# Two places a piece in the weight ring between the layers of a two-layer decode kernel

## The chip, the core and the metric

The kernel runs on one core of one Trainium2 chip. The metric is device time in microseconds (us) of one execution.

## The reference

One token for each of two sequences (B = 2, model width 576) goes through attention, MLP, attention, MLP. Both attentions read the same key and value caches and the same weights, and both MLPs the same weights; everything is float32.

```python
# x (2, 1, 576); k_cache, v_cache (2, 32, 8192, 128); wq (576, 4096); wo (4096, 576)
# w_gate, w_up (576, 4608); w_down (4608, 576)
def attention(x):                      # on layernorm(x)
    q = (x @ wq) as 32 heads of 128
    p = softmax(q . k_cache * 128 ** -0.5)
    return (p . v_cache) as 4096 @ wo
def mlp(x):                            # on layernorm(x)
    return (gelu(x @ w_gate) * (x @ w_up)) @ w_down
x = x + attention(layernorm(x)); x = x + mlp(layernorm(x))      # layer 0
x = x + attention(layernorm(x)); x = x + mlp(layernorm(x))      # layer 1
```

## The kernel before

**What is moved.** The two caches hold 537 MB together and are read in each layer, so the kernel is a stream of about 1.15 GB from HBM into one big on-chip tile, `space`. An item is the keys, or the values, of two heads (or of one head for the last four items): 128 partitions by 64 KB or 32 KB. VectorE multiplies keys by the query (L560), GpSimd adds the halves of each product (L577), VectorE sums them (L580), ScalarE takes the exponential (L634), and TensorE multiplies the weights of the softmax by the values (L675). Layer 1 walks the items backwards, and the last keys and values of layer 0 stay on the chip for it.

**Who orders the transfers.** All of them are issued by SyncE in one written order. `plan_first`, `plan_mlp` and `plan_second` append one closure a transfer to `queue`; `pump` lets the head of the list issue as long as `Arena` finds room for it, and `done(key)` frees a piece and calls `pump`. All of this happens while the program is built: in the running program it becomes a semaphore wait in SyncE's queue, in that order, for the instruction that read the old content last.

**The ring.** Between the two streams of caches most of `space` is taken by the held items. Left over are four places of 2304 floats a partition (9216 bytes; 1.18 MB over 128 partitions), which `Arena.ring` hands out in turn. Through these go, in order: `wo` of layer 0 (eight pieces, TensorE L728), the first MLP's gate and up weights (L844), its down weights (L895), and `wq` of layer 1 (L508). Then come keys and values again. In the kernel before, every one of these pieces takes one place, whatever its length up to 2304 floats.

**The first MLP before (`split`).** `norm(split=True)` lays x out so that `split_products(h)` can do half of the 4608 columns at a time: nine pieces for h = 0 (four of gate, one of both, four of up), then `activate(0)`, then nine for h = 1, then `activate(1)`. Each gate or up piece is two DMAs of 64 partitions by 9216 bytes (`split_rows`, L237) or four of 4608 bytes (`split_middle`, L247). The second MLP, at the end, has the whole of `space` and uses `half_rows` (L227) and `all_products` (L858): rows cut in two halves, nine half rows a partition for each of gate and up, both halves of the columns accumulated at once in the two halves of the PSUM tile `acc`. The down weights come in eight pieces of four rows (L260) and one of the four remaining rows (L264).

**TensorE's clock.** TensorE's granted clock in the trace is 1.0 or 0.5. In the last MLP `idle_products` puts products whose result nobody reads between the pieces of the down weights (`IDLE`, L304; L821).

**Names that the steps below use.** `norm` L465, `add_to_x` L497, `attention` L501, `mlp` L826, `activate` L864; tiles `acc`, `bank`, `bank2`, `kept` (PSUM), `prz` (softmax weights), `xt` (transposed x), `hT` (result of the activation).

Of the kernel before, what the change touches and what calls it, by code (L numbers as in the profile page):

```python
# [15 lines left out]
P = 128  # L16
# [51 lines left out]
class Arena:  # L68
# [31 lines left out]

    def ring(self, key, n):

        at = self.take(key, RING + self.turn % NPLACE * PLACE, n)
        self.turn += at is not None
        return at

    def fit(self, key, n, lo=0):
# [15 lines left out]
def decode_layers(ctx, tc, x_in, kc, vc, wq, wo, wg, wu, wd, out):  # L123
# [28 lines left out]
    def done(key):  # L152
        arena.free(key)
        pump()
# [73 lines left out]

        weights(key, len(us) * width, first, transfers)

    def split_rows(name, w, h, u):

        rows = w[:, DF // 2 * h:DF // 2 * (h + 1)].rearrange("(m r) w -> m r w", r=NU)

        def transfers(t):
            for e in range(2):
                nc.sync.dma_start(t[e::2, :], rows[:, 5 * e + u, :])  # L237

        weights((name, 0, h, u), DF // 2, None, transfers)

    def split_middle(h):

        def transfers(t):
            for g, w in enumerate((wg, wu)):
                for e in range(2):
                    lo, n = DF // 4 * (2 * h + e), DF // 4
                    nc.sync.dma_start(  # L247
                        t[e::2, n * g:n * (g + 1)], w[:, lo:lo + n].rearrange("(m r) w -> m r w", r=NU)[:, 4, :]
                    )

        weights(("gu", 0, h), DF // 2, None, transfers)

    def down(layer, rows):

        (t0, i0), (t1, i1) = rows[0], rows[-1]
# [23 lines left out]
    def out_rows(layer, g):  # L279
# [9 lines left out]
        weights(("wo", layer, g), GH * D, whole_at[layer], transfers)  # L289


    single = [range(u, u + 1) for u in range(NU)]
    three = [range(u, u + 3) for u in range(0, NU, 3)]
    WQ = [three, single]
    GU = [three, three[:-1] + single[-3:]]

    DOWN = [
        [[(t, i) for i in range(lo, lo + 4)] for t in range(NT) for lo in (0, 4)] + [[(t, NI - 1) for t in range(NT)]],
        [[(t, i) for i in range(NI)] for t in range(NT - 2)]
        + [[(NT - 2, i) for i in range(lo, hi)] for lo, hi in ((0, 5), (5, 9))]  # L300
        + [[(NT - 1, i) for i in range(lo, hi)] for lo, hi in ((0, 3), (3, 6), (6, 8), (8, 9))],
    ]

    IDLE = (4, 4, 2, 2, 1)  # L304

    whole_at = (None, 0)
    def groups(layer):
# [68 lines left out]
            out_rows(1, g)  # L376

    def plan_mlp(layer):
        if layer == 0:
            for h in range(2):  # L380
                for u in range(4):
                    split_rows("g", wg, h, u)
                split_middle(h)
                for u in range(4):
                    split_rows("u", wu, h, u)
        else:
            for g, (name, w) in enumerate((("g", wg), ("u", wu))):
                for us in GU[g]:
                    half_rows((name, layer, us[0]), w, us, 0)
        for rows in DOWN[layer]:  # L390
            down(layer, rows)

# [44 lines left out]
    )  # L437

    xt = consts.tile([P, PAD + NU * 32], F32, name="xt")
    nc.vector.memset(xt, 0.0)

# [18 lines left out]
        return smalls[0][0:p, 0:n]  # L462


    def norm(split=False):  # L465
# [11 lines left out]
        xr = x.rearrange("p (m r) -> p r m", r=NU)  # L477
        xs = xc.rearrange("p w s -> p (w s)")
        if split:
            xm = xs[:, :5 * 32].rearrange("p (u m e) -> p u m e", u=5, e=2)  # L480
            parts = [(xm[:, 0:4, :, e], xr[:, 5 * e:5 * e + 4, :], 0) for e in range(2)]
            parts += [(xm[:, 4, :, e], xr[:, 4, :], e) for e in range(2)]
            xs = xs[:, :5 * 32].rearrange("p (u q) -> p u q", u=5)
        else:
            parts = [(xc[:, :, s], x, s) for s in range(2)]
            xs = xs.rearrange("p (q u) -> p u q", u=NU)
        for to, of_x, s in parts:
            nc.vector.tensor_scalar(to, of_x, mv[:, 0:1], side[:, s:s + 1], op0=ALU.subtract, op1=ALU.mult)
        u = xs.shape[1]
        nc.vector.transpose(xt[:, PAD:PAD + 32 * u].rearrange("p (u q) -> p u q", u=u), xs)  # L490
# [7 lines left out]
        nc.vector.tensor_add(x, xps, x)  # L498


    def attention(layer):  # L501
        rstd = norm()

        for us in WQ[layer]:
            w = ready.pop(("wq", layer, us[0])).rearrange("p (u c w) -> p u c w", c=4, w=EQ)
            for u in us:
                for c in range(4):
                    nc.tensor.matmul(  # L508
                        acc[32 * c:32 * c + 2 * B, 0, :], xt[:, PAD + 32 * u:PAD + 32 * u + 2 * B],
                        w[:, u - us[0], c, :], start=(u == 0), stop=(u == NU - 1),  # L510
                    )
            done(("wq", layer, us[0]))
        qsb = once.tile([P, EQ], F32, name="qsb", tag="row")

        qb, S, prod, rs, mT, tot, rinv, osb = {}, {}, {}, {}, {}, {}, {}, {}
# [300 lines left out]
            project(g)  # L816
        add_to_x()

    def idle_products(n):
        for _ in range(n):  # L820
            nc.tensor.matmul(  # L821
                kept.rearrange("p j d -> p (j d)")[0:4, :HG], ident[:, 0:4], xt[:, :HG], start=True, stop=True,
            )


    def mlp(layer):  # L826
        split = layer == 0
        rstd = norm(split)
        hT = once.tile([P, 2, NI, 2, 2, B], F32, name="hT", tag="xc")

        def window(u, at):

            return xt[:, PAD + 32 * u - at:PAD + 32 * u - at + 4 * B]

        def split_products(h):

            steps = [(("g", layer, h, u), u, 2, (0,)) for u in range(4)] + [(("gu", layer, h), 4, 1, (0, 1))]
            steps += [(("u", layer, h, u), u, 2, (1,)) for u in range(4)]
            for key, u, sides, gs in steps:
                w = ready.pop(key).rearrange("p (k c w) -> p k c w", c=4, w=HG)  # L840
                for k in range(2):
                    g, e = (k, 0) if u == 4 else (gs[0], k)
                    for c in range(4):
                        nc.tensor.matmul(  # L844
                            acc[32 * c:32 * c + 4 * B, h, :HG], window(u, 4 * g + 2 * e), w[:, k, c, :],
                            start=(key == steps[0][0] and k == 0), stop=(key == steps[-1][0] and k == 1),
                        )
                done(key)

        def all_products():  # L850

            for g, name in enumerate("gu"):
                for us in GU[g]:
                    w = ready.pop((name, layer, us[0])).rearrange("p (u v c w) -> p u v c w", v=2, c=4, w=HG)
                    for u in us:
                        for v in range(2):
                            for c in range(4):
                                nc.tensor.matmul(  # L858
                                    acc[32 * c:32 * c + 4 * B, v, :HG], window(u, 4 * g), w[:, u - us[0], v, c, :],
                                    start=(g == 0 and u == 0), stop=(g == 1 and u == NU - 1),  # L860
                                )
                    done((name, layer, us[0]))

        def activate(v):  # L864

# [13 lines left out]
            nc.vector.tensor_scalar_mul(to[:, :, 0, :], a, 0.5)  # L879
            nc.scalar.mul(to[:, :, 1, :], a, 0.5)  # L880

        if not split:
            all_products()
        for v in range(2):
            if split:
                split_products(v)
            activate(v)
        for n, rows in enumerate(DOWN[layer]):
            if layer == 1 and n < len(IDLE):
                idle_products(IDLE[n])  # L890
            w = ready.pop(("d", layer, rows[0])).rearrange("p (i c) -> p i c", c=D)
            for k, (t, i) in enumerate(rows):
                v, e = divmod(t, 2) if split else (t % 2, t // 2)
                for c in range(4):
                    nc.tensor.matmul(  # L895
                        xps[32 * c:32 * c + 2 * B, :], hT[:, v, i, e, :, :].rearrange("p s b -> p (s b)"),
                        w[:, k, c * CW:(c + 1) * CW],
                        start=(rows is DOWN[layer][0] and k == 0), stop=(t, i) == (NT - 1, NI - 1),
                    )
            done(("d", layer, rows[0]))  # L900
# [35 lines left out]
```

## Time and profile before

| what | value |
|---|---|
| median of three executions | 2691.84 us (2690.37 to 2692.72) |
| profiled execution | 2692.85 us |
| its span, first to last instruction | 2691.1 us |
| read from HBM | 1153.18 MB, 429 GB/s over the span |
| busy: TensorE, VectorE, GpSimd, ScalarE | 34%, 69%, 45%, 5% |
| chain that ended last | DMA 85%, VectorE 12% |
| mean granted TensorE clock | 0.629 |

The time around the span, 1.75 us, is in the profiled execution's time and not in its span. The traced execution stands 1.0 us above the median. The page divides the span into 40 slices of 67 us; the change lies in slices 19 to 21, from about 1260 to 1420 us. The granted clock is a record of its own in the trace, in stretches whose lengths are multiples of 3.41 us.

### The profile page before, as it was taken

What the parts mean: (1) busy time and instruction counts of PE and PEld (TensorE: products, weight loads), DVE (VectorE), ACT (ScalarE), POOL (GpSimd) and SP (SyncE); (2) the same over time, 40 slices, a digit from 0 to 9 for tenths busy, and PEclk for the clock granted to TensorE, in tenths of its full rate; (3) what the DMA queues carried; (4) which work ended last, traced back from release to release, by engine and by line L of the source; (5) the groups of instructions that cost most, each with busy time, mean ns of one, the idle gap of its engine ahead of it and who ended that gap; (6) DMA issues with size and microseconds to landing.
All of it is one profiled execution on the core that took longest, in us unless ns stands there. A gap on an engine that the chain in (4) does not pass through costs nothing.

```text
span 2691.1 us, 18230 instructions
## 1 busy us (share of the span) xinstructions
PE 923.9 (34%) x7046; PEld 300.5 (11%) x7046; DVE 1851.1 (69%) x1688; ACT 144.6 (5%) x736; POOL 1214.7 (45%) x550
## 2 busy tenths in 40 slices
PE   1323332332233233334654333233233323332346
PEld 0100010000001010111211101001010101010022
DVE  4877787678777776867038778777777877787740
ACT  0000000000000000000016000000000000000000
POOL 2644454455445444544018554445444544454420
PEclk7656655665666566666766665666566556656678
DMA  9999999999999999999999999999999999999998
GB/s 421 435 437 433 432 432 433 431 436 433 432 436 432 434 427 434 433 430 425 408 402 425 433 435 429 436 430 433 436 433 432 431 437 432 431 433 435 434 421 368
DMA packets 33831, 1154.36 MB, mean 429 GB/s; under 512 B 4024, under 2 KB 4048, under 8 KB 5840
## 3 DMA queue, kind: packets, MB, share of 16 engines
q1 hardware_dynamic: 33704, 1153.19, 99.7%
q8 instruction: 55, 0.90, 0.1%
q14 instruction: 32, 0.26, 0.0%
q10 hardware_dynamic: 40, 0.01, 0.0%
HBM read 1153.18 MB, written 0.00 MB: 429 GB/s over the span
## 4 chain that ended last, share of the span: by engine, by line
DMA 85%; DVE 12%; PE 1%; POOL 1%; ACT 1%; issue 1%; SPq 0%; ACTq 0%; POOLq 0%; DVEq 0%
DMA space<-in_A_k_cache_dram 77%; DVE space L560 7%; DVE S L580 4%; DMA space<-in_B_w_up_dram 2%; DMA space<-in_B_w_down_dram 2%; DMA space<-in_A_v_cache_dram 1%; DMA space<-in_A_wo_dram 1%; DMA space<-in_B_w_gate_dram 1%; POOL space L577 1%; DMA space<-in_A_wq_dram 1%; ACT space L570 0%; POOL space L564 0%; DMA x<-in_A_x_dram 0%; PE bank L895 0%; PE acc L844 0%
## 5 line engine op out<-in xcount | busy, mean ns | idle before, releaser
L577 POOL TENSOR_TENSOR space<-space 128x1024 f32<-128x1024 f32 (+1 forms) x510 | 1181.4, 2316 | 1208.0 <-DVE space L560 1197.3
L560 DVE TENSOR_TENSOR space<-space,bank 128x2048 f32<-128x2048 f32 (+1 forms) x512 | 1153.7, 2254 | 608.4 <-DMA space<-in_A_k_cache_dram 574.8
L675 PE MATMUL acc<-space,prz 128*8 128x512 f32 x4096 | 596.6, 746 | 451.9 <-DMA space<-in_A_v_cache_dram 447.8
L580 DVE TENSOR_REDUCE S<-space 128x16 f32<-128x1024 f32 (+1 forms) x512 | 610.1, 1192 | 3.5 <-POOL space L577 3.3
L528 PE MATMUL bank<-qsb,pick 4*64 4x128 f32 (+1 forms) x256 | 46.6, 437 | 776.5 <-DVE space L560 773.8
L675 PEld LDWEIGHTS acc<-space,prz 128*8 128x8 f32 x4096 | 119.2, 104 | 872.0 <-DMA space<-in_A_v_cache_dram 450.0
L632 ACT ACTIVATE nbs<-bank 64x1 f32<-64x1 f32 (+1 forms) x128 | 21.1, 165 | 2256.5 <-PE bank L611 2255.8
L528 PEld LDWEIGHTS bank<-qsb,pick 4*64 4x64 f32 (+1 forms) x256 | 20.9, 202 | 835.0 <-DVE space L560 803.7
L700 PE MATMUL bank<-of,osb 128*32 128x2 f32 x512 | 40.9, 202 | 130.9 <-DVE osb L691 130.9
L611 PE MATMUL bank<-m,unit 1*128 1x2 f32 (+1 forms) x136 | 39.0, 354 | 129.2 <-DVE m L609 129.2
L494 POOL TENSOR_TENSOR rstd<-ve,mhalf 128x1 f32<-128x1 f32 x4 | 2.2, 552 | 167.5 <-DVE ve L492 167.5
L691 DVE SCALAR_TENSOR_TENSOR osb<-acc,diag,osb 128x128 f32<-128x128 f32 x192 | 67.4, 351 | 6.8
L869 DVE STREAM_TRANSPOSE o<-o 128x288 f32<-128x288 f32 x4 | 2.8, 690 | 94.4 <-ACT o L867 94.4
L642 PE MATMUL bank<-sums,unit 128*128 128x2 f32 x120 | 35.3, 363 | 92.0 <-ACT prz L634 92.0
L700 PEld LDWEIGHTS bank<-of,osb 128*32 128x32 f32 x512 | 35.8, 154 | 139.5 <-DVE osb L691 137.9
L634 ACT ACTIVATE prz<-S,nbs 64x128 f32<-64x128 f32 (+1 forms) x128 | 50.7, 396 | 12.4 <-POOL prz L624 8.3
L603 PE MATMUL bank<-ident,m 128*1 128x128 f32 x68 | 24.9, 366 | 73.8 <-DVE m L601 73.7
L611 PEld LDWEIGHTS bank<-m,unit 1*128 1x128 f32 x136 | 33.2, 301 | 148.7 <-DVE m L609 148.7
L570 ACT ACTIVATE space<-space 128x128 f32<-128x128 f32 x164 | 48.3, 296 | 18.1 <-DVE space L560 16.1
L498 DVE TENSOR_TENSOR x<-bank,x 128x144 f32<-128x144 f32 x4 | 1.2, 308 | 69.3 <-PE bank L895 39.9
L564 POOL TENSOR_TENSOR space<-space,qs 128x512 f32<-128x512 f32 x24 | 30.5, 1272 | 26.7 <-ACT qs L559 26.2
L642 PEld LDWEIGHTS bank<-sums,unit 128*128 128x128 f32 x120 | 30.1, 312 | 97.2 <-ACT prz L634 97.2
(70 smaller groups left out, 381.7 us busy)
## 6 DMA issues: line engine op xcount, KB each, us to landing
space<-in_A_v_cache_dram SPq DMA_DIRECT2D x8, 4096.0 KB
space<-in_A_k_cache_dram SPq DMA_DIRECT2D x6, 4096.0 KB
space<-in_A_wo_dram SPq DMA_DIRECT2D x15, 1152.0 KB
space<-in_A_k_cache_dram SPq DMA_DIRECT2D x15, 1024.0 KB
space<-in_B_w_down_dram SPq DMA_DIRECT2D x9, 1152.0 KB
space<-in_B_w_gate_dram SPq DMA_DIRECT2D x3, 3456.0 KB
space<-in_A_v_cache_dram SPq DMA_DIRECT2D x10, 1024.0 KB
space<-in_A_wq_dram SPq DMA_DIRECT2D x3, 3072.0 KB
```

The source lines that it names most:

```text
L528: nc.tensor.matmul(qb[n][to, :], pick[32 * c:32 * c + 4, r:r + 1].to_broadcast([4, P // it.heads]), qsb[32 * c:32 * c + 4, (h % 4) * DH:(h ...
L560: nc.vector.tensor_tensor(out=u[:, :rows, :], in0=t[:, :rows, :], in1=qb[n].unsqueeze(1).to_broadcast([P, rows, DH]), op=ALU.mult)
L564: nc.gpsimd.tensor_tensor(out=u[:, rows:, :], in0=t[:, rows:, :], in1=q.unsqueeze(1).to_broadcast([P, JC - rows, DH]), op=ALU.mult,)
L570: nc.scalar.activation(u[:, j, :], u[:, j, :], AF.Copy, accum_out=S[n][:, k * JC + j:k * JC + j + 1])
L577: nc.gpsimd.tensor_tensor(out=half, in0=half, in1=u[:, :r, DH // 2:], op=ALU.add)
L580: nc.vector.tensor_reduce(out=S[n][:, k * JC:k * JC + own_rows(n, k)], in_=prod.pop((n, k)), axis=AX.X, op=ALU.add)
L611: nc.tensor.matmul(mT[n][:, :heads], ones[0:1, :], m1[:, :heads], start=True, stop=True)
L634: nc.scalar.activation(pr[at, lo:].rearrange("p (g e) -> p g e", e=4)[:, 0:it.rows // 2:2, :], s[at, :it.rows].rearrange("p (g r) -> p g r ...
L642: nc.tensor.matmul(tot[n][:, :ITEMS[n].heads], ones, rs.pop(n), start=True, stop=True)
L675: nc.tensor.matmul(accumulator(n)[32 * c:32 * c + 8, :], pr[:, at:at + 8], t[g // 4][:, g % 4 * 4:g % 4 * 4 + 4, :].rearrange("p j d -> p ...
L691: nc.vector.scalar_tensor_tensor(t, q[:, r, :], diag[:, r:r + 1], t, op0=ALU.mult, op1=ALU.add,)
L700: nc.tensor.matmul(po[lo:lo + 32, i, :], t[:, i::GH], of, start=True, stop=True)
```

## The change

- `Arena.ring` takes as many places in a row as a piece needs and moves the turn by as many; it asserts that a piece does not run over the ring's end.
- The first MLP is no longer split. It uses `half_rows` and `all_products` as the second one does, with pieces of two half rows (18432 bytes a partition, two places, one DMA) and one of a single half row for gate, and a single one and four of two for up. Both `activate` calls follow after all products.
- Its down weights come in four pieces of eight rows (two places) and one of the four remaining rows.
- `wq` of layer 1 comes in pieces of 1, 1, 1, 2, 2, 1, 1 half rows instead of nine single ones.
- `idle_products` moves its result from `kept` to a part of `bank2` and reads `prz` (256 columns) instead of `xt` (288 columns). It is called in more places: three after the norm of the first MLP, two after each of seven of its two-row pieces, 3, 2, 2, 2 before its first four down pieces, three after the norm of the second attention, and one after each piece of `wq` but the last. The second MLP's calls stay.

```diff
     def ring(self, key, n):
-        at = self.take(key, RING + self.turn % NPLACE * PLACE, n)
-        self.turn += at is not None
+        k, m = self.turn % NPLACE, -(-n // PLACE)
+        assert k + m <= NPLACE
+        at = self.take(key, RING + k * PLACE, n)
+        if at is not None:
+            self.turn += m
         return at
...
-    def split_rows(name, w, h, u):
...
-    def split_middle(h):
...
-    WQ = [three, single]
-    GU = [three, three[:-1] + single[-3:]]
+    WQ = [runs(3, 3, 3), runs(1, 1, 1, 2, 2, 1, 1)]
+    GU = [[runs(2, 2, 2, 2, 1), runs(1, 2, 2, 2, 2)], [runs(3, 3, 3), runs(3, 3, 1, 1, 1)]]
     DOWN = [
-        [[(t, i) for i in range(lo, lo + 4)] for t in range(NT) for lo in (0, 4)] + [[(t, NI - 1) for t in range(NT)]],
+        [[(t, i) for i in range(NI - 1)] for t in range(NT)] + [[(t, NI - 1) for t in range(NT)]],
...
-    IDLE = (4, 4, 2, 2, 1)
+    IDLE = [(3, 2, 2, 2), (4, 4, 2, 2, 1)]
...
+    def idle_products(n):
+        for _ in range(n):
+            nc.tensor.matmul(
+                bank2[0:4, 2 * GH:2 * GH + 2 * P], ident[:, 0:4], prz.rearrange("p a e -> p (a e)")[:, :2 * P],
+                start=True, stop=True,
+            )
...
     def attention(layer):
         rstd = norm()
+        if layer == 1:
+            idle_products(3)
...
             done(("wq", layer, us[0]))
+            if layer == 1 and us[-1] < NU - 1:
+                idle_products(1)
...
     def mlp(layer):
-        split = layer == 0
-        rstd = norm(split)
+        rstd = norm()
+        if layer == 0:
+            idle_products(3)
...
                     done((name, layer, us[0]))
+                    if len(us) == 2 and us[-1] < NU - 1:
+                        idle_products(2)
...
-        if not split:
-            all_products()
+        all_products()
         for v in range(2):
-            if split:
-                split_products(v)
             activate(v)
         for n, rows in enumerate(DOWN[layer]):
-            if layer == 1 and n < len(IDLE):
-                idle_products(IDLE[n])
+            if n < len(IDLE[layer]):
+                idle_products(IDLE[layer][n])
...
-                v, e = divmod(t, 2) if split else (t % 2, t // 2)
+                v, e = t % 2, t // 2
```

More of the change, by code (lines that the diff above doesn't have):

```diff
@@ L229, in half_rows @@
         weights(key, len(us) * width, first, transfers)
-    def split_rows(name, w, h, u):
[L233 to L239, printed above, removed]
-    def split_middle(h):
[L243 to L251, printed above, removed]
     def down(layer, rows):
@@ L289, in out_rows, with runs @@
         weights(("wo", layer, g), GH * D, whole_at[layer], transfers)
-    single = [range(u, u + 1) for u in range(NU)]
-    three = [range(u, u + 3) for u in range(0, NU, 3)]
-    WQ = [three, single]
-    GU = [three, three[:-1] + single[-3:]]
+    def runs(*sizes):
+        at = [sum(sizes[:k]) for k in range(len(sizes) + 1)]
+        return [range(lo, hi) for lo, hi in zip(at, at[1:])]
+    WQ = [runs(3, 3, 3), runs(1, 1, 1, 2, 2, 1, 1)]
+    GU = [[runs(2, 2, 2, 2, 1), runs(1, 2, 2, 2, 2)], [runs(3, 3, 3), runs(3, 3, 1, 1, 1)]]
     DOWN = [
-        [[(t, i) for i in range(lo, lo + 4)] for t in range(NT) for lo in (0, 4)] + [[(t, NI - 1) for t in range(NT)]],
+        [[(t, i) for i in range(NI - 1)] for t in range(NT)] + [[(t, NI - 1) for t in range(NT)]],
         [[(t, i) for i in range(NI)] for t in range(NT - 2)]
@@ L378, in plan_mlp @@
     def plan_mlp(layer):
[L379 to L389, printed above, removed]
+        for (name, w), pieces in zip((("g", wg), ("u", wu)), GU[layer]):
+            for us in pieces:
+                half_rows((name, layer, us[0]), w, us, whole_at[layer])
         for rows in DOWN[layer]:
@@ L462, in small, with norm @@
         return smalls[0][0:p, 0:n]
-    def norm(split=False):
+    def norm():
         stats = work.tile([P, 6], F32, name="stats")
@@ L476, in norm @@
         xc = once.tile([P, CW, 2], F32, name="xc", tag="xc")
-        xr = x.rearrange("p (m r) -> p r m", r=NU)
-        xs = xc.rearrange("p w s -> p (w s)")
-        if split:
[L480 to L490, printed above, removed]
+        for s in range(2):
+            nc.vector.tensor_scalar(
+                xc[:, :, s], x, mv[:, 0:1], side[:, s:s + 1], op0=ALU.subtract, op1=ALU.mult,
+            )
+        xs = xc.rearrange("p w s -> p (w s)").rearrange("p (q u) -> p u q", u=NU)
+        nc.vector.transpose(xt[:, PAD:].rearrange("p (u q) -> p u q", u=NU), xs)
         ve = work.tile([P, 1], F32, name="ve")
@@ L498, in add_to_x @@
         nc.vector.tensor_add(x, xps, x)
+    def idle_products(n):
[3 more added lines that the diff above has]
+                start=True, stop=True,
+            )
     def attention(layer):
         rstd = norm()
+        if layer == 1:
+            idle_products(3)
         for us in WQ[layer]:
@@ L817, in attention @@
         add_to_x()
[L819 to L823, printed above, removed]
     def mlp(layer):
-        split = layer == 0
-        rstd = norm(split)
+        rstd = norm()
+        if layer == 0:
+            idle_products(3)
         hT = once.tile([P, 2, NI, 2, 2, B], F32, name="hT", tag="xc")
@@ L833, in window @@
             return xt[:, PAD + 32 * u - at:PAD + 32 * u - at + 4 * B]
[L835 to L848, printed above, removed]
         def all_products():
             for g, name in enumerate("gu"):
-                for us in GU[g]:
+                for us in GU[layer][g]:
                     w = ready.pop((name, layer, us[0])).rearrange("p (u v c w) -> p u v c w", v=2, c=4, w=HG)
@@ L880, in activate @@
             nc.scalar.mul(to[:, :, 1, :], a, 0.5)
-        if not split:
-            all_products()
+        all_products()
         for v in range(2):
-            if split:
-                split_products(v)
             activate(v)
         for n, rows in enumerate(DOWN[layer]):
-            if layer == 1 and n < len(IDLE):
-                idle_products(IDLE[n])
+            if n < len(IDLE[layer]):
+                idle_products(IDLE[layer][n])
             w = ready.pop(("d", layer, rows[0])).rearrange("p (i c) -> p i c", c=D)
             for k, (t, i) in enumerate(rows):
-                v, e = divmod(t, 2) if split else (t % 2, t // 2)
+                v, e = t % 2, t // 2
                 for c in range(4):
```

## The prediction

> **What bounds the kernel now.** I read the page first (rows 2 and 4), then the stretches between the layers, then TensorE's and SyncE's rows there.
>
> ```profile
> span 2691.1 us, 18230 instructions
> DMA  9999999999999999999999999999999999999998
> GB/s 421 435 437 433 432 432 433 431 436 433 432 436 432 434 427 434 433 430 425 408 402 425 433 435 429 436 430 433 436 433 432 431 437 432 431 433 435 434 421 368
> DMA 85%; DVE 12%; PE 1%; POOL 1%; ACT 1%; issue 1%; SPq 0%; ACTq 0%; POOLq 0%; DVEq 0%
> ```
>
> The DMA engines are never idle, and the caches stream at about 433 GB/s. Only slices 19 to 21 dip. There, in stretches (time and length, busy times by engine, granted clock, DMA share, GB/s; the last line is undisturbed streaming):
>
> ```profile
> 1284.00:1297.00 13.00, 7.53 (x134) 4.14 (x138) 2.44 (x10) 0.00 (x0) 0.06 (x1) 0.72 1.01 391
> 1297.00:1345.00 48.00, 30.41 (x288) 7.68 (x281) 1.84 (x7) 1.03 (x4) 0.50 (x1) 0.72 1.01 416
> 1345.00:1376.00 31.00, 19.45 (x306) 9.38 (x310) 4.27 (x15) 0.91 (x3) 0.55 (x1) 0.65 1.01 417
> 1376.00:1394.00 18.00, 11.32 (x62) 1.16 (x54) 0.03 (x1) 1.11 (x3) 0.00 (x0) 0.74 1.00 403
> 1394.00:1420.00 26.00, 8.69 (x41) 2.87 (x41) 21.41 (x19) 16.81 (x109) 18.83 (x15) 0.59 0.97 368
> 700.00:1100.00 400.00, 127.16 (x842) 38.22 (x846) 300.04 (x260) 13.12 (x60) 195.63 (x83) 0.60 1.00 433
> ```
>
> The dips look like a gain waiting to be had: against 433 they come to 13 x 42/433 + 48 x 17/433 + 31 x 16/433 + 18 x 30/433 + 26 x 65/433 = 9.4 us. Most of it is not there. Each transfer is split over 16 DMA engines, and the trace records 16 completions. For the `wo` piece at 1284 the first came at 1277.62, the last at 1284.29; at the end of `wq` they are 1 us apart (1389.82, 1390.79). So the fast engines lose a 6.7 us lead, while a piece counts as landed with the engine that is last. That engine's completions follow each other without a hole until 1378.14; up to 1391 it then loses 0.26 us once. What can be won is small; what counts is whether the last engine runs dry.
>
> TensorE's rows show how a ring place is turned around (start, length, idle before):
>
> ```profile
> 1337.51 2.11 PE L844 MATMUL acc<-space,xt 128*8 128x288 f32 x16 [0.66 <-DMA space<-in_B_w_up_dram]
> 1340.29 2.11 PE L844 MATMUL acc<-space,xt 128*8 128x288 f32 x16 [0.67 <-DMA space<-in_B_w_up_dram]
> 1343.08 1.73 PE L844 MATMUL acc<-space,xt 128*8 128x288 f32 x16 [0.69 <-DMA space<-in_B_w_up_dram]
> ```
>
> A piece lands each 2.78 us, and TensorE needs 2.11 us for it at clock 0.5 (1.16 at 1.0, the row at 1301.13). Three pieces are queued behind it, 8.3 us, so SyncE's issue is never late.
>
> **The change, part by part.** Differences are against the profiled 2692.85 us.
>
> *Larger packets: -1.2 us.* A packet of 9216 bytes takes a mean 351 ns on its engine, one of 27648 bytes (the last MLP's) 1030 ns; on the line between them one of 18432 takes 691 ns against 702 for two. Eight packets an engine make a two-place piece 5.47 us instead of 5.56; 12 such pieces save 1.1 us, the two of `wq` 0.1. If the price per byte stayed, 0. SyncE issues 32 gate and up DMAs and 8 quarter ones as 10, and 8 of down as 4; its issue (0.33 to 0.6 us each) runs beside transfers, so nothing.
>
> *The turnaround with two places: +1.0 us.* After a piece's last completion come 0.14 us to TensorE's start, the products (2.32 us at clock 1.0, 4.22 at 0.5), 0.05 to SyncE, 0.33 of issue, and 1.36 until an engine with nothing queued delivers: at 1375.40 an issue ended, 1379.27 was the first completion, eight 314 ns packets are 2.51. Together products + 1.88. Cover is now one piece, 5.47 us, where it was three. At clock 1.0 this takes 4.20 and fits; at 0.5 it takes 6.10, and the DMA engines stand still for 0.63 us. The products may take 3.59 us.
>
> So the clock decides. The trace's clock record changes on a grid of 3.41 us. Against TensorE's busy share in each step: of 196 full steps, those followed by a full one were at least 41% busy, those followed by a half one had a median of 21% and three quarters of them at most 35%. Of 585 half steps the 81 followed by a full one were at least 76% busy. The idle products (0.50 us each by L821: four instructions, two products of 288 columns, 1.13 us, scaled to 256) make TensorE's burst 2.32 + 1.0 = 3.3 of each 5.47 us; the gap is 2.1. A step that holds the gap whole is 38% busy, under 41%; by the places at which it can start this is 27% of the steps, 0.44 a period. The step after it is at half clock and catches what is left of the next products: short by 0.63 to 0, 0.2 in the mean. Twelve refills x 0.44 x 0.2 = 1.0. Bounds: 0 (always full) and 12 x 0.63 = 7.6 (always half).
>
> The Trainium skill (TensorE: Matmul & The Clock Gate, Part 1) says the clock falls to half after an idle window of about 3.4 us and rises after a busy one. By it a 2.1 us gap never costs the clock, this term would be 0 and the sum +0.4 us. The steps here disagree: half of the full steps after which the clock fell were 21% busy or more.
>
> *Both activations at the end: +0.4 us.* One takes 2.9 us (1319.25 to 1322.15, L867 to L880) and the first was hidden behind the second half's products. Now TensorE's first down piece waits for it: with the last up piece landing at T, at full clock at T + 0.14 + 2.32 + 0.06 + 2.9 = T + 5.4, when that piece lands anyway (T + 5.47). Cost 0; at half clock the refill behind it is late by 2.4 us. The second activation ends at T + 8.4, before its piece lands at T + 10.9. Near the full end, since three idle products keep TensorE busy there.
>
> *The norm before `wq`: +0.5 us.* Place 3 holds the first `wq` piece, so the two-row piece of places 2 and 3 can't be queued across the norm: three places, 7.45 us, instead of four. From the last down piece: 0.14 + 1.2 products + 3.4 norm (1369.76 to 1373.12) + 1.1 + 1.74 = 7.6 us at full clock, 9.3 at half. Bounds 0.15 and 1.9; the three idle products favour the first.
>
> *The norm before gate: 0.* The unsplit one takes 3.4 us instead of 3.1, but the first gate piece now lands 5.47 us after the last `wo` (1292.64), at 1298.1, after the norm (1297.1). Before, TensorE waited there for the norm. The idle products wait for VectorE's read of `bank2` (L475); behind them stands only that gate piece. Uncovered they would cost 1.5 us.
>
> *Idle products between the `wq` pieces: -0.3 us.* The last piece's products took 1.69 us, near half clock; at full clock the query is 0.6 us earlier, and the 368 GB/s of 1394 to 1420 starts there. I take half; bounds -0.6 and 0. In the second MLP an idle product is 11% shorter; only if the clock fell at 2672 to 2689 would the tail's last three products (0.92 us for a piece) cost 0.7. I take 0.
>
> *Instruction fetches: +1.0 us.* Seven 16 KB fetch packets of 1.1 us fall on single engines between 1282 and 1376. So far they met engines with a lead of some us. With the ring just covered there is little lead, and a fetch delays a landing by about 0.6 us (the sharing engine moves 16 KB in that). Bounds 0 and 4; I take two.
>
> Sum: -1.2 + 1.0 + 0.4 + 0.5 - 0.3 + 1.0 = **+1.4 us**. From the median, 2691.84, this gives **2693.2 us**. What can be told from no change here is about 0.2%, 5.4 us: the forecast is no change.
>
> **Rivals.**
> *The refill comes late for most of the stage (slower).* Its place is the refill of a two-place piece; it decides once products and latency together pass 5.47 us, that is with products over 3.59 us or a latency 1.3 us longer than 1.36. For it: the stage ran at 0.72 and 0.65, the spare is only 1.27 us at full clock, and idle products queued at half clock (2 us) make TensorE itself need 6.2 of 5.47 us. Price at half clock: 7.6 + 2.4 + 1.9 - 1.2 = +10.7, 2702.5 us; with half the refills late, +6. Against it: that much work is over 76% busy, which brought the full clock back. 0.30.
> *The clock stays full.* A step that holds the gap is 38% busy, hardly under 41%, and a little more idle work would keep the clock. Then each refill has 1.27 us to spare, which also swallows the fetches: -1.2 + 0.15 - 0.6 = -1.7, 2690.2 us. Against it: at 0.72 the stage has lost it often so far. 0.13. The Trainium skill's rule above would have it so.
> *The dips are worth their whole rate (faster).* If fewer, larger transfers ran the stretches from 1284 to 1394 at 433 GB/s, 5.5 us, and the query came 0.6 earlier: 2685.7 us. Against it: the last engine had no holes to give back. 0.04.
> *The packets are no cheaper*, the change does not do what its size promises: +2.6, 2694.4 us. 0.05.
> The forecast has the rest, 0.48.
>
> **How the numbers follow.** Faster by over 0.2% is the third rival alone, 0.04. Slower is the first, 0.30. Same is the rest: 0.48 + 0.13 + 0.05 = 0.66. The range reaches down past the full clock to 2689.0, which leaves out the third rival, and up to 2703.0, which takes in the late refill at its price and leaves out some 0.12 where latency and fetches come on top. The likeliest case's own range is 2690 to 2697.
>
> **What would show it.** In the trace of after: gate, up and down pieces landing each 5.5 us; TensorE's row for one of them 2.3 us, some 3 to 4.2; the last engine's completions without holes, or with holes under 0.7 us; `wq` complete within 3 us of 1390.8. A granted clock near 1.0 in 1297 to 1376 would speak for the second rival, holes at most pieces for the first. I am wrong if the stretches before 1260 or after 1450 change by more than 1 us, as nothing there is touched.

## The result, and the profile after

| | before | after |
|---|---|---|
| median of six executions each | 2692.28 us (2690.37 to 2693.25) | 2703.73 us (2702.24 to 2706.32) |
| profiled execution | 2692.85 us | 2706.32 us |
| its span | 2691.1 us | 2704.5 us |

The change makes the kernel slower: ratio 1.0043, 95% interval 1.0032 to 1.0053, or 11.4 us by the medians. The forecast was no change. The profiled execution of after is the slowest of its six, so what the trace shows of the loss (13.4 us of span) is some 2 us more than the median's.

The page of after, the same rows as before:

```profile
span 2704.5 us, 18292 instructions
DMA  9999999999999999999999999999999999999998
GB/s 419 435 434 434 434 431 435 432 434 434 434 434 434 431 432 433 435 428 416 367 367 418 435 434 433 434 433 433 433 433 433 434 433 433 433 433 434 433 423 373
DMA 85%; DVE 11%; PE 2%; POOL 1%; ACT 1%; issue 1%; SPq 0%; ACTq 0%; POOLq 0%; DVEq 0%
```

Slices 20 and 21 move 367 GB/s where they moved 408 and 402; the two beside them lose 9 and 7, and the others stand within a few GB/s. The row of DMA shares shows none of this: a share of 0.93 is still a 9.

The stretches of after, with the columns of the prediction's table (length, busy times by engine, granted clock, DMA share, GB/s):

```profile
1284.00:1297.00 13.00, 7.92 (x138) 4.17 (x135) 2.37 (x8) 0.00 (x0) 0.00 (x0) 0.76 0.97 372
1297.00:1345.00 48.00, 30.13 (x264) 9.94 (x266) 0.05 (x2) 0.00 (x0) 0.55 (x1) 0.78 0.93 373
1345.00:1376.00 31.00, 19.57 (x274) 9.55 (x262) 3.69 (x14) 1.82 (x6) 0.00 (x0) 0.81 0.86 339
1376.00:1394.00 18.00, 10.60 (x134) 4.57 (x134) 2.42 (x8) 0.00 (x0) 0.55 (x1) 0.91 0.97 373
1394.00:1420.00 26.00, 10.73 (x60) 2.80 (x60) 11.52 (x9) 8.44 (x51) 7.72 (x6) 0.70 0.98 382
700.00:1100.00 400.00, 125.86 (x834) 37.92 (x838) 300.00 (x259) 13.13 (x60) 195.58 (x83) 0.61 1.00 433
```

Gate and up (1297 to 1345) fell from 416 to 373 GB/s, down (1345 to 1376) from 417 to 339, although TensorE's clock rose from 0.72 and 0.65 to 0.78 and 0.81. The last `wq` piece lands at 1405.48 instead of 1390.79, 14.7 us later; from there to the end of the span it is 1299.0 us instead of 1300.3. The undisturbed stretch stays at 433.

The chain that ended last shows how the loss comes about (start, length, what; the longest pieces):

```profile
1293.99 10.84 DMA space<-in_B_w_gate_dram
1304.88 3.35 PE acc L817 x32
1308.24 10.71 DMA space<-in_B_w_gate_dram
1319.00 3.80 PE acc L817 x32
1322.82 7.79 DMA space<-in_B_w_up_dram
1330.65 4.07 PE acc L817 x32
1334.74 9.10 DMA space<-in_B_w_up_dram
1343.88 3.50 PE acc L817 x32
1347.40 11.05 DMA space<-in_B_w_down_dram
```

Transfers and products take turns in it: a piece lands, its products run, and only then is the piece issued that ends the next link. With L853 for down, TensorE's products hold 18.7% of the chain between 1284 and 1420. With a ring of two pieces that loop is tight: two pieces take 11 us to move, and a link of the chain (10.71 + 3.35, say) takes 14.

TensorE's rows for the two-row pieces (start, length, tile and shapes, idle before and its releaser):

```profile
1299.13 2.13 PE L817 MATMUL acc<-space,xt 128*8 128x288 f32 x32 [0.72 <-DMA space<-in_B_w_gate_dram]
1304.88 3.32 PE L817 MATMUL acc<-space,xt 128*8 128x288 f32 x32 [2.79 <-DMA space<-in_B_w_gate_dram]
1311.65 3.27 PE L817 MATMUL acc<-space,xt 128*8 128x288 f32 x32 [2.11 <-DMA space<-in_B_w_gate_dram]
1330.65 4.03 PE L817 MATMUL acc<-space,xt 128*8 128x288 f32 x32 [4.92 <-DMA space<-in_B_w_up_dram]
1343.88 3.45 PE L817 MATMUL acc<-space,xt 128*8 128x288 f32 x32 [4.65 <-DMA space<-in_B_w_up_dram]
```

A piece takes 2.1 us at full clock and 3.3 to 4.0 when the clock falls, and TensorE waits 2 to 5 us for the next. By the record of completions the two-row pieces of gate and up land, from the second on, 5.8, 6.8, 7.4, 6.1, 5.5, 7.7 and 5.5 us after the piece ahead of each, where 5.49 us is what one takes undisturbed.

The completions of the 16 engines, recorded for each transfer, say which pieces lose. The records do not name the engines; I take the last completion of one transfer and that of the next to be the same engine's. What lies between the two beyond the transfer's own 5.49 us (2.78 for a single place) I call a hole. The end of the issue plus 1.36 us is the time at which the transfer could reach an engine with nothing queued; an engine that had completed the transfer ahead by then had run dry. Four transfers of after, in us:

| issued | could reach an engine | transfer ahead complete, first and last engine | first engine dry for | own first and last completion | hole |
|---|---|---|---|---|---|
| 1301.31 (gate) | 1302.99 | 1302.52, 1304.83 | 0.47 | 1308.57, 1311.60 | 1.28 |
| 1308.24 (gate) | 1309.93 | 1308.57, 1311.60 | 1.36 | 1315.48, 1318.95 | 1.86 |
| 1347.40 (down) | 1349.09 | 1347.58, 1349.32 | 1.51 | 1354.78, 1358.46 | 3.65 |
| 1351.55 (down) | 1353.24 | 1354.78, 1358.46 | 0 | 1360.87, 1363.98 | 0.03 |

From gate to `wq` the holes are 15.6 us in after (about 6.5 in gate and up, 6.5 in down, 2.7 in `wq`) and 0.7 in before. Of these 15.6 only 0.7 us is the last engine itself with nothing queued. But in nine of the 23 transfers the *first* engine had run dry, by up to 3.5 us, and these nine hold 12.3 us, 1.37 each; the other 14 hold 0.24 each.

### The profile page after: what moved, and what is told of

Its sections match the earlier page's. It is cut to its first block, busy times and chain, and to the rows that moved or that the text cites. A ratio compares the mean times of both kernels' runs of the same rounds, so it can differ in the third digit from the quotient of the medians.

```text
span 2704.5 us, 18292 instructions
## 1 busy us (share of the span) xinstructions
PE 930.8 (34%) x7116; PEld 308.5 (11%) x7116; DVE 1851.1 (68%) x1686; ACT 144.5 (5%) x736; POOL 1214.0 (45%) x550
## 4 chain that ended last, share of the span: by engine, by line
DMA 85%; DVE 11%; PE 2%; POOL 1%; ACT 1%; issue 1%; SPq 0%; ACTq 0%; POOLq 0%; DVEq 0%
DMA space<-in_A_k_cache_dram 76%; DVE space L539 7%; DVE S L559 4%; DMA space<-in_B_w_up_dram 2%; DMA space<-in_A_wo_dram 2%; DMA space<-in_B_w_down_dram 2%; DMA space<-in_A_v_cache_dram 1%; DMA space<-in_B_w_gate_dram 1%; DMA space<-in_A_wq_dram 1%; PE acc L817 1%; POOL space L556 1%; ACT space L549 1%; PE bank L853 0%; DMA x<-in_A_x_dram 0%; PE acc L485 0%
## 5 line engine op out<-in xcount | busy, mean ns | idle before, releaser
L817 PE MATMUL acc<-space,xt 128*8 128x288 f32 x576 | 53.1, 527 | 39.6 <-DMA space<-in_B_w_up_dram 21.1
```

The source lines that it names most:

```text
L817: nc.tensor.matmul(acc[32 * c:32 * c + 4 * B, v, :HG], window(u, 4 * g), w[:, u - us[0], v, c, :], start=(g == 0 and u == 0), stop=(g == 1 ...
```

## The experiments

Four theories stood against each other.
- **A, the late refill.** A two-place piece is freed only when its last engine has landed and all its products are done. The fast engines were through 2 to 3 us earlier and run dry, even where the last one doesn't; each restart costs.
- **B, the clock.** The refill is late only because the clock falls; at full clock it fits.
- **C, the large transfers.** Transfers of 18432 bytes a partition are slower in themselves, whenever they are issued.
- **D, the unsplit MLP.** Both activations at the end, the longer norm and the idle products cost the time.

Each kernel was timed against the kernel before on the same chip (medians of before 2692.0 to 2693.0).

### One place a piece and one idle product a piece, the rest as changed (e1_single)

```diff
-    WQ = [runs(3, 3, 3), runs(1, 1, 1, 2, 2, 1, 1)]
-    GU = [[runs(2, 2, 2, 2, 1), runs(1, 2, 2, 2, 2)], ...
+    WQ = [runs(3, 3, 3), runs(1, 1, 1, 1, 1, 1, 1, 1, 1)]
+    GU = [[runs(1, 1, 1, 1, 1, 1, 1, 1, 1), runs(1, 1, 1, 1, 1, 1, 1, 1, 1)], ...
-        [[(t, i) for i in range(NI - 1)] for t in range(NT)] + ...
+        [[(t, i) for i in range(lo, lo + 4)] for t in range(NT) for lo in (0, 4)] + ...
-    IDLE = [(3, 2, 2, 2), ...
+    IDLE = [(3, 1, 1, 1, 1, 1, 1, 1), ...
-                    if len(us) == 2 and us[-1] < NU - 1:
-                        idle_products(2)
+                    if layer == 0 and us[-1] < NU - 1:
+                        idle_products(1)
```

> The kernel after, but every ring piece one place again (single half rows of gate, up and wq; four rows of down); the MLP stays unsplit, one idle product after each gate or up piece and before the down pieces. Theory A, late refill (two places leave one piece of cover, the DMA engines run dry at the refills, and each restart costs the last of the 16 engines 0.3 to 3.6 us): all of it goes, 2691 to 2694 us, no holes of the last engine before 1376. Theory C (a 2.36 MB transfer with 18432-byte packets is slow in itself): the same, 2691 to 2694. Theory D (the unsplit MLP's activations and the norm stand on the path): stays 3 to 5 us above before, 2695 to 2698.

Measured: 2692.83 us (2691.28 to 2693.77), ratio 1.0 (0.999 to 1.0009). Its stretches of gate and up, and of down:

```profile
1297.00:1345.00 48.00, 29.91 (x327) 9.70 (x326) 0.49 (x2) 0.47 (x1) 0.56 (x1) 0.96 1.01 422
1345.00:1376.00 31.00, 18.56 (x338) 9.54 (x339) 6.13 (x22) 1.36 (x6) 0.55 (x1) 1.00 1.01 417
```

The rate is back at 422 and 417 GB/s, and the holes are 0.3 us in all. The whole loss hangs on the places a piece takes; D falls. The clock is nearly full here, and still the kernel is no faster than before: a full clock by itself brings nothing.

### Which stage: gate and up alone, down alone (e7_gu_two, e6_before_down8)

The first is after with `wq` and down in single places as in e1, so that gate and up alone take two. The second is the kernel before with the new `ring` and down in eight rows.

> The kernel after with two-place pieces for gate and up alone; down and wq in single places. In the trace of after the gate and up pieces held 7 us of the holes, down 6.5, wq 3. Theory A, additive by piece: 2697 to 2701. If only the place of the activation and the norm matter (Theory D), 2693 to 2695.

> The kernel before (split MLP, single wq rows, no idle products between the layers) with only the down weights of the first MLP in pieces of eight rows and two places. In the trace of after the four down pieces held 6.5 us of the last engine's 20 us of holes, with idle products. Theory A: 4 to 8 us slower than before, 2696 to 2701. If a two-place piece costs only what the prediction's sum gave it (0.1 to 0.3 us each), 2692 to 2694.

Measured: 2698.02 us for gate and up (ratio 1.0017, 1.0007 to 1.0026) and 2696.53 for down (1.0013, 1.0004 to 1.0023), so about +5 and +4. Together that is 9 of the 11.4 us; the large pieces of each stage cost time without those of the other. (By the count above the holes of after are 15.6 us, not the 20 of the second expectation.) Not all of it lies in the large pieces themselves: of the holes 4.5 us in the first and 2.3 in the second are in the single places behind them. The stretch of gate and up of the first, whose profiled execution took 2703.19 us and so lost 5 us more than its median, and that of down of the second:

```profile
1297.00:1345.00 48.00, 25.23 (x248) 8.82 (x248) 0.00 (x0) 0.00 (x0) 0.37 (x1) 0.83 0.90 365
```

```profile
1345.00:1376.00 31.00, 15.91 (x290) 10.08 (x290) 3.75 (x14) 0.67 (x3) 0.00 (x0) 0.72 0.98 377
```

### The clock: no idle products, and five a piece (e3_no_idle, e4_five_idle)

```diff
 # e3: every call of idle_products between the layers is taken out
 # e4:
-                        idle_products(2)
+                        idle_products(5)
-    IDLE = [(3, 2, 2, 2), ...
+    IDLE = [(5, 5, 5, 5), ...
```

> The kernel after without any of the idle products between the layers (those of the second MLP stay). Theory B, the clock (the refills are late because TensorE is at half clock): the granted clock between 1297 and 1376 falls from about 0.8 to under 0.65, products of a piece take 4.2 us, each refill is 1 us later, 2708 to 2714 us. Theory A expects the same direction, 2705 to 2712. If idle products hold up the pieces behind them, it is faster than after, under 2702.

> The kernel after with five idle products instead of two after a two-row gate or up piece and instead of 3, 2, 2, 2 before the down pieces, so that TensorE is busy enough to keep the full clock. Theory B: granted clock over 0.9 from 1297 to 1376, refill 4.2 us after a landing, holes gone, 2691 to 2694 us. Theory A: at full clock the refill is still only 1.3 us ahead, less than the lead that the fast engines have over the last one, so restarts go on: 2696 to 2701 us.

Measured: 2705.49 us without (ratio 1.0046, 1.0031 to 1.0061) and 2700.65 us with five (1.0028, 1.0017 to 1.0038). Gate and up, then down, first without, then with five:

```profile
1297.00:1345.00 48.00, 24.63 (x240) 7.33 (x244) 0.14 (x2) 0.00 (x0) 0.56 (x1) 0.68 0.91 362
1345.00:1376.00 31.00, 15.58 (x248) 7.88 (x240) 3.67 (x14) 1.82 (x6) 0.00 (x0) 0.68 0.89 347
```

```profile
1297.00:1345.00 48.00, 36.92 (x332) 14.12 (x330) 1.06 (x4) 0.00 (x0) 0.55 (x1) 0.90 0.97 392
1345.00:1376.00 31.00, 21.43 (x365) 12.09 (x366) 5.32 (x20) 1.83 (x6) 0.00 (x0) 1.00 0.99 401
```

The third column from the right shows what the edit does: a clock of 0.68 without, 0.90 and 1.00 with five. The last column shows what that is worth: at full clock down still moves 401 GB/s and not 417, and by the medians 3 of 11 us come back. Within gate, up and down it is worth more than that: in the profiled executions their holes are 5.6 us with five where after had 13, while `wq`, which the edit leaves as it was, went from 2.7 to 4.1. Without idle products the clock fell to 0.68, not under 0.65, and the time is in the range that A gave it, not in B's. B falls: a clock near full does not make the refill fit. The clock matters only as part of the products' time.

### The products' time: a quarter of the strips, a quarter of the columns (e2_quarter, e5_quarter_width)

```diff
 # e2, first MLP only
-                            for c in range(4):
+                            for c in range(4 if layer else 1):
 # e5, first MLP only (gate and up; the products of down likewise)
-                                    acc[32 * c:32 * c + 4 * B, v, :HG], ..., w[:, u - us[0], v, c, :],
+                                    acc[32 * c:32 * c + 4 * B, v, :HG if layer else HG // 4], ...
```

> The kernel after with its two-place pieces, but in the first MLP only one of the four column strips of each product is computed (gate, up and down), so that TensorE needs a quarter of the products for a piece and the refill is issued 2 to 3 us earlier; the output is not the reference's. The transfers are those of after. Theory A: gate, up and down pieces land each 5.5 us with holes of the last engine under 3 us in all instead of 14, and only wq keeps its holes: 2692 to 2697 us. Theory C: the pieces stay slow, 2701 to 2704 us.

> The kernel after with its transfers as they are, but each product of the first MLP runs over a quarter of its columns (72 instead of 288, 36 instead of 144); the other columns are left out, so the output is not the reference's. This does what computing one strip of four did not do: a two-row piece takes TensorE about 0.6 to 0.9 us instead of 2.1 to 4.2. Theory A, late refill: the refill is issued 1.5 to 3 us earlier, gate, up and down lose at most 3 us instead of 12, wq keeps its 2 to 4 us: 2693 to 2698 us. Theory C, large transfers are slow in themselves: nothing changes, 2701 to 2704 us.

The first was to make the products short and didn't. A row of it, beside two rows of the second:

```profile
1298.87 2.10 PE L817 MATMUL acc<-space,xt 128*8 128x288 f32 x8 [1.65 <-DMA space<-in_B_w_gate_dram]
```

```profile
1309.86 1.15 PE L817 MATMUL acc<-space,xt 128*8 128x72 f32 x32 [2.96 <-DMA space<-in_B_w_gate_dram]
1338.07 0.69 PE L817 MATMUL acc<-space,xt 128*8 128x72 f32 x32 [2.66 <-DMA space<-in_B_w_up_dram]
```

Eight products on one of the four column strips took 2.10 us, as 32 on all four did (2.13): the strips run side by side. So its 2701.9 us (ratio 1.0033, 1.002 to 1.0046) tests nothing. With a quarter of the columns the products take 0.7 to 1.15 us, and the time is 2696.11 us (1.0009, 1.0000 to 1.0018). Gate and up, and down:

```profile
1297.00:1345.00 48.00, 20.21 (x318) 9.74 (x319) 0.00 (x0) 0.15 (x1) 0.34 (x1) 0.62 1.00 419
1345.00:1376.00 31.00, 15.10 (x321) 6.65 (x320) 6.09 (x22) 1.67 (x6) 0.55 (x1) 0.67 0.98 396
```

The same large transfers move at 419 GB/s in gate and up, at a clock of only 0.62, with no engine dry and 0.7 us of holes there. C falls, and B once more. What stays is behind that: 3 us of holes in `wq`, whose products were not shortened (its first pair found the first engine dry for 2.8 us and lost 1.4; a single piece behind the pairs lost 1.7), and 2.3 in two pieces of down.

### Single places, but fewer of them (e9_two_of_four, e10_three_of_four)

```diff
 # both on top of e1; e9, then e10
-        k, m = self.turn % NPLACE, -(-n // PLACE)
+        k, m = self.turn % (2 if key[0] in ("g", "u", "d") else NPLACE), -(-n // PLACE)
+        k, m = (self.turn + 1) % 3 if key[0] in ("g", "u", "d") else self.turn % NPLACE, -(-n // PLACE)
```

> The kernel with single-place pieces everywhere (the one that came out at 2692.8 us), but the first MLP's pieces use only two of the ring's four places, so that one piece of 2.78 us covers a refill, with packets of 9216 bytes. Theory A: products 1.16 us at full clock and 1.88 us for the refill are 3.04 us against 2.78, so the engines run dry at each of 27 pieces: 0.3 us each at least, 0.9 with the restart, 2700 to 2720 us. Theory C (only large transfers are slow): 2692 to 2695 us.

> The version with single places throughout (2692.8 us), but the pieces of the first MLP use only three of the four places of the ring, in turn. Two pieces are queued behind a refill, 5.56 us, nearly the 5.49 us of the changed kernel; the products of a piece take 1.16 us at full clock, so the refill is issued some 1.7 us after a landing and delivers 3.0 us after it. Late refill (A), by which the spread of the 16 engines (2 to 3 us) is what the spare must hold: spare 5.6 - 3.0 = 2.5 us, 2692.5 to 2698, well below the 2715 of two places of four. If cover alone decided, whatever the products take, the time would be that of the changed kernel, 2701 to 2704.

Measured: two places 2715.14 us (ratio 1.0078, 1.0063 to 1.0093), three places 2698.0 us (1.0021, 1.0012 to 1.0031), at the upper end of what A gave it. Gate and up, two places and then three:

```profile
1297.00:1345.00 48.00, 27.78 (x254) 8.05 (x251) 0.00 (x0) 0.00 (x0) 0.55 (x1) 0.84 0.87 318
```

```profile
1297.00:1345.00 48.00, 31.95 (x296) 9.77 (x298) 0.87 (x3) 0.00 (x0) 0.55 (x1) 0.83 0.94 372
```

Small transfers lose as well, 22 us, when the cover is 2.78 us. With three places the cover is 5.56 us, as in after, but the products are half as long, and the loss is half of after's. The profiled execution, 2701.31 us, lies 3 us above the median. Of its 8 us of holes 2.6 follow the norm before gate, where a refill left the first engine dry for 4.4 us, and 2.3 lie where down's products wait for `hT`; only 3 us are of the ring's steady turn. Cover alone doesn't decide; cover less all that TensorE does or waits for does.

### The changed kernel with two DMAs a piece (e8_two_dmas)

```diff
-            nc.sync.dma_start(t.rearrange("p (u w) -> p u w", w=width), rows[:, us[0]:us[-1] + 1, :])
+            to = t.rearrange("p (u w) -> p u w", w=width)
+            if len(us) == 2:
+                for k in range(2):
+                    nc.sync.dma_start(to[:, k:k + 1, :], rows[:, us[k]:us[k] + 1, :])
+            else: ...
 # and for the eight rows of down
+                    for k in range(0, 8, 4): nc.sync.dma_start(to[:, k:k + 4, :], src[:, 0, k:k + 4, :])
```

> The changed kernel with its pieces, places, turn, idle products and unsplit MLP, but each two-place piece is loaded by two DMAs, one for each place (two half rows as two DMAs of 9216 bytes a partition; eight down rows as two of four rows; the wq pairs likewise). Each place is then refilled as soon as its own products are done, with three places (8.3 us) queued behind it, as before. Late refill (A): 2692 to 2696, the 11 us gone, with no holes of the last engine in gate, up and down. If instead something in the way the ring frees or orders two places, the unsplit products or the idle products cost the time: 2701 to 2704 as in the changed kernel.

Measured: 2691.87 us (2690.85 to 2694.79), ratio 1.0001 (0.9992 to 1.001). The 11 us are gone. Gate and up, down, and three of TensorE's rows:

```profile
1297.00:1345.00 48.00, 30.67 (x320) 9.74 (x312) 0.00 (x0) 0.00 (x0) 0.16 (x1) 0.89 1.01 423
1345.00:1376.00 31.00, 22.30 (x338) 10.87 (x340) 6.12 (x22) 1.82 (x6) 0.55 (x1) 0.87 1.01 414
```

```profile
1303.95 1.16 PE L827 MATMUL acc<-space,xt 128*8 128x288 f32 x16 [1.62 <-DMA space<-in_B_w_gate_dram]
1306.73 1.16 PE L827 MATMUL acc<-space,xt 128*8 128x288 f32 x16 [0.78 <-DMA space<-in_B_w_gate_dram]
1309.51 1.16 PE L827 MATMUL acc<-space,xt 128*8 128x288 f32 x16 [1.62 <-DMA space<-in_B_w_gate_dram]
```

The products of a piece are now two groups of 16, each started by its own transfer, one each 2.78 us, and each place is refilled after its own group. Holes: 0.3 us in all, the spread between first and last engine a steady 2.9 us through up and the first pieces of down. The ring's new code, the unsplit products and the idle products are all still there and cost nothing. This is the change's own kernel without the late refill and without the large transfers; that the latter are not the cause was seen with a quarter of the columns, so A stands. It is not faster than before, and no version here was.

## Why the prediction was wrong

**The step that failed** is in the reading of what bounds the kernel: "the fast engines lose a 6.7 us lead, while a piece counts as landed with the engine that is last", so that "what counts is whether the last engine runs dry". The first half is right, the second is not. The last engine hardly ran dry, 0.7 us in all, where the sum gave 1.0. But it lost 15 us in its own transfers, four fifths of it in those that found the fast engines dry. The refill was measured against 5.47 us, the cover of the last engine. It should have been measured against that of the first, which is shorter by the spread, 2.3 to 3.5 us in gate. On that clock the refill is late at full TensorE clock too: 4.2 us after the landing, against 5.5 less 2.3 to 3.5. The other kernels agree (spread is the median one of the transfers of gate and up; holes are those of gate and up in the profiled execution, before 0.3):

| kernel | cover, us | products of one wait, us | refill delivers (products + 1.88) | spare | spread | holes | median over before, us |
|---|---|---|---|---|---|---|---|
| e1, e8 | 8.3 | 1.16 to 2.11 | 3.0 to 4.0 | 4.3 to 5.3 | 3.2, 2.9 | 0.1, 0.0 | 0 |
| quarter columns (e5) | 5.5 | 0.7 to 1.15 | 2.6 to 3.0 | 2.5 to 2.9 | 1.8 | 1.0 | 3 |
| three places (e10) | 5.56 | 1.16 to 2.11 | 3.0 to 4.0 | 1.6 to 2.6 | 1.9 | 4.5 | 6 |
| after | 5.5 | 2.1 to 4.0 | 4.0 to 5.9 | -0.4 to 1.5 | 2.6 | 6.5 | 11 |
| two places (e9) | 2.78 | 1.16 to 2.11 | 3.0 to 4.0 | -1.2 to -0.3 | 0.7 | 13.4 | 22 |

With the spare above the spread of first and last engine little or nothing is lost; about at the spread some, and below it the loss grows. e9, with smaller pieces, pays at twice as many refills: 19 found the first engine dry, 1.0 us each, and in these the last engine itself had nothing queued for 5.0 us in all. That the loss starts with the first of the 16 engines, and not with the second or third, is read from these spreads; no run separates them.

**Term by term.** *Turnaround, +1.0, and fetches, +1.0:* these were the mis-sized terms. Gate, up and down together held 13 us of holes where the two gave 2. Their bounds together (7.6 and 4) come near it, but for a reason the working doesn't have: the 7.6 was the last engine at half clock throughout, and the clock was 0.78 and 0.81. Six fetches at the 0.1 to 0.3 us found below are 0.6 to 1.8 of the 13, so the turnaround is the larger miss. The parts of the turnaround were right one by one: products 2.13 at full clock (2.32 forecast), latency 1.36 (issue done at 1301.63, first completion at 1308.57, less a piece of 5.49, is 1.45). *Larger packets, -1.2:* right; a packet of 18432 bytes has a median of 0.686 us, against 0.691 forecast, though no time here shows the gain. *Activations, +0.4:* 0. The first was done at 1354.5 and its down piece landed only at 1358.46. *Norm before gate, 0:* right. *Norm before `wq`, +0.5:* the first pair behind it lost 1.3 us, inside the bounds; all of `wq` lost 2.7. *Idle products between `wq` pieces, -0.3:* from the last landing to the end it was 1.3 us shorter, but that stretch runs from 1297.6 to 1300.8 us over all kernels and is 1299.6 without any idle products (e3), so nothing is shown for them.

**The rivals.** The time is that of the first rival, 2702.5, and its place was right: the refill of a two-place piece. Its condition was met only in part: of the eleven two-place pieces of gate, up and down whose products stand in a row of their own, four passed its 3.59 us (3.78, 4.03, 4.02, 3.68), and its price asked for half clock throughout. That the time agrees is luck, since what it priced, the last engine standing still, came to 0.7 us. The range, up to 2703.0, ended 0.7 us below the median because I let its price be its ceiling. The second rival, a full clock at which everything fits, was nearly reached in e4 and cost 8 us.

**The clock.** The reading that it falls after a step that is part idle was right. TensorE's idle times before 1304.88 and 1311.65 are 2.79 and 2.11 us, and in the clock's own record it fell at 1305.65 and 1312.48. The steps of 3.41 us that ended there were 23% and 38% busy, both under the 41% of the working. The Trainium skill (TensorE: Matmul & The Clock Gate, Part 1) asks for an idle window of about 3.4 us; both gaps are shorter, so the trace disagrees here.

**What stays open** is how the last engine, which had work queued, comes to lose about 1 us in a transfer at whose start the others had none. Part of it is instruction fetches, which the prediction had in its sum: packets of 16 KB, 0.9 to 1.1 us on one engine, six of them from 1284 to 1400. Over the nine kernels that lost time, the holes from gate to `wq`, without the time in which the last engine itself had nothing queued, sort like this (a fetch counts as in a transfer if it overlaps the time since the last completion ahead):

| transfers | no fetch in them | with a fetch |
|---|---|---|
| first engine not dry | 0.12 us each (161) | 0.41 us each (37) |
| first engine dry | 0.89 us each (52) | 1.02 us each (23) |

A fetch adds 0.1 to 0.3 us; e1 and e8 have as many fetches and 0.3 us of holes in all, so it is the lost lead that lets them through. The dry start is worth nearly 0.8 us by itself, but only as a mean: the loss hardly follows how long the first engine was dry (0.65 us each in the 18 transfers dry for up to 0.5 us, 0.96 in the 14 dry for over 2 us), and single dry starts cost nothing, as the one of 0.64 us in before (`wq`, issued at 1375.07) and two of 0.35 and 0.43 us in e8. Of the cause only the place is shown: of ten packets that start within 0.2 us of each other at such a restart, seven or eight take about 1.4 to 1.6 us and the rest 1.0 to 1.4, instead of 0.69 (at 1323.8, 1335.8 and 1348.4). That the engines hinder each other when they restart together is only argued.

## What to carry to other kernels

In a ring like this one, hold the refill against the cover of the *first* DMA engine to finish, that is the cover less the spread between first and last completion, and let "no engine dry" be the aim, not "the last engine is not dry". Two places moved by one DMA halve the steps in which they come free: if the larger piece is wanted, issue one DMA a place, so that each place waits for its own products only. A transfer that bounds the kernel and has no holes gets nothing from larger packets beyond their own price, here about 1 us of 2692 by the packets' times.

## What the runs showed of the hardware

- The 16 engines stand up to 7 us apart under a steady queue (6.7 at the end of `wo` in before, 2.9 in up in e8), and that lead is a buffer: with it, 21 packets from 1284 to 1400 in e8 that took 0.45 us or more beyond the median of their size (12.6 us beyond it in sum) cost the pieces 0.3 us in all.
- A higher clock is worth something only where it shortens a wait that counts: from 0.68 (e3) to 0.90 and 1.00 (e4) the time fell by 4.8 us, where the refill was late; e1 at 0.96 and 1.00 and before at 0.72 and 0.65, where it was not, take the same time.
- Products on one column strip of four take as long as on all four (2.10 and 2.13 us).
